# Two fillers fewer at the start, a k step of four more blocks ahead of a transpose, and token tiles 8-11 taken in pairs for three feature blocks

## The chip, the cores and the metric

The kernel runs on one NeuronCore of a Trainium2 chip. The metric is the device time of one execution in microseconds; the time given for a kernel is the median of its runs. The core's engines are TensorE (PE, matrix multiplication, with PEld for the loading of its stationary operand), VectorE (DVE), ScalarE (ACT), GpSimd (POOL) and SyncE (SP, which issues most DMAs).

## The reference

The layer adds three things: the input, a linear attention block and a dense GELU block, both fed by the same layernorm.

```python
def _A_ref(x, wqkv, wo):                      # x: 1 x 2048 x 640, 32 heads of 20
    qkv = (x @ wqkv) ...                      # q, k, v
    phi = lambda t: jnp.where(t > 0, t + 1, jnp.exp(t)) + 1e-6
    pq, pk = phi(q), phi(k)
    kv = einsum("bhsd,bhse->bhde", pk, v);  z = einsum("bhsd->bhd", pk)
    o = einsum("bhqd,bhde->bhqe", pq, kv) / (einsum("bhqd,bhd->bhq", pq, z) + 1e-6)
    return o.reshape(B, S, D) @ wo
def _B_ref(x, w1, b1, w2, b2):                # w1: 640 x 1536, w2: 1536 x 640
    return gelu(x @ w1 + b1) @ w2 + b2
xn = layernorm(x)
return x + _A_ref(xn, A_wqkv, A_wo) + _B_ref(xn, B_w1, B_b1, B_w2, B_b2)
```

All arrays are bfloat16. There are 2048 tokens, so 16 token tiles of 128; the model width of 640 makes 5 k steps of 128 (`DT`), and the hidden width of 1536 makes 12 feature blocks of 128 (`JT`).

## The kernel before

A planner (`Planner`) records, for every engine, its instructions in the order in which the Python code issues them, and puts semaphore waits where one depends on another. So each engine, and each DMA queue (most transfers go through SP's), works strictly in the order of the source[...]. PSUM is used as a ring of eight banks: `take(1)` hands out the next one, `at(b)` sets the ring, and a unit of matmuls has to wait until the bank's former content is read.

**Start (lines 442-459).** `filler(n, w)` issues n matmuls of constants, w columns wide, whose results nobody reads: four of 512 columns first, then six matmuls (L445) that open banks 0 to 5 with a matmul of constants summing to zero, then six fillers of 128 columns. Meanwhile DVE and POOL compute the layernorm of token tile 0: `ln_half` (L351, statistics), `ln_aggr` (L359 on DVE, the power on POOL at L361) and `ln_norm` (L373). `transp2(0)` (L336) transposes tile 0 on PE, `copy2(0)` brings it to `xnT`, one part on ACT (L344), the other on DVE (L345).

**First product, xn @ W1 (lines 461-512).** A list `plan` orders the work on PE. Its entries are:

- `hk(t, n, jb, ks)` (L431): for n tiles from tile t, feature block jb and only the k steps in `ks`; used for tiles 0 and 1, whose 12 feature blocks stay open in banks 0 to 5, so that work can begin when only some of the weights W1 and one tile are there. The last k step of an odd block is followed by two GELUs on ACT (L438).
- "B1": a small transpose of the bias. "T1": the transposes of tile 1 (L336) and their copies, and then on DVE the statistics of tiles 2 and 3. "T2": the transposes of tile 2 (`transp`, L381), its copy on DVE (L389), `ln_norm(3)`, the transposing DMA of tile 3, and then `ln_rest`, which holds all the remaining layernorms (tiles 4 to 15) and the loads of x for tiles 8 to 15.
- `pack(t, ...)`, that is `h_pack` (L415): one tile, four feature blocks in one bank. `h_list(t, n, lo, hi)`, that is one `h_unit` (L400) for each feature block from lo to hi: n tiles from t at once, so matmuls n x 128 columns wide, five k steps, and one GELU (L404).

Tiles 3 to 15 are transposed not on PE but by a DMA on SP's queue (`xnT_dma`, L263), issued as soon as the tile is normalised. An `h_unit` waits for the transposed form of all the n tiles that it takes.

**After that.** The k projection and its positive map phi (L548, L554), the sums over tokens (L581, L590), the q projection (L634), the small products for kv and the denominators (L644 to L698), and the output (`out_mm` L755, `rem_mm` L766), whose results DVE adds to x and DMAs write out.

Of the kernel before, what the change touches and what calls it, by code (L numbers as in the profile page):

```python
# [7 lines left out]
P = 128  # L8
# [104 lines left out]
def bass_parallel_sum__linear_attn_block__dense_activation_gelu__prompt_kernel(  # L113
# [9 lines left out]
    JT = F // P  # L123
# [17 lines left out]
    with contextlib.ExitStack() as es:  # L141
# [59 lines left out]
        def take(n):  # L201
            b = ring[0]
            if n == 2 and b % 2:
                b += 1
            b %= 8
            ring[0] = (b + n) % 8
            return b

        def bank(b, lo=0, hi=512):
            return ps[:, b * 512 + lo: b * 512 + hi]  # L210
# [106 lines left out]
        def filler(n, w=512):  # L317
            b = take(1)
            Pl.ins(pe, [lambda e: e.matmul(bank(b, 0, w), nc.const_aps.tensor(1.0, [P, P], BF16),
                                           nc.const_aps.tensor(1.0, [P, w], BF16), start=True, stop=True)  # L320
                        for _ in range(n)], writes=[B_[b]])
# [25 lines left out]
        def ln_half(t, h):  # L347
            s = t % 4
            cut = XA if t == 0 else HW
            lo, hi = ((0, cut), (cut, D))[h]  # L350
            Pl.ins(v, lambda e: e.bn_stats(stats[:, s, 6 * h:6 * h + 6], x_in[:, t, lo:hi]),  # L351
                   reads=[r_x[t][min(h, len(r_x[t]) - 1)]], writes=[r_stats[s][h]])
            if h == 0:
                Pl.ins(g, lambda e: e.tensor_single_scalar(stats[:, s, 2:3], stats[:, s, 2:3], D * EPS, ALU.add),
                       reads=[r_stats[s][0]], writes=[r_stats[s][0]])
# [68 lines left out]
        def at(b):  # L424
            ring[0] = b
# [14 lines left out]
                        reads=[B_[b], r_b1c], writes=[r_HG[u][jb - 1 + i] for u in range(t, t + n)])  # L440

        at(6)
        filler(4)
        for b in range(6):
            Pl.ins(pe, lambda e, b=b: e.matmul(  # L445
                bank(b), nc.const_aps.tensor(1.0, [P, P], BF16), pm[:].broadcast_to((P, 512)), start=True, stop=False),
                reads=[r_pm], writes=[B_[b]])
        at(7)
        filler(6, P)
        ln_half(0, 0)  # L450
        ln_half(0, 1)
        ln_aggr(0)
# [8 lines left out]
        h_list = lambda t, n, lo, hi: [(t, n, jb) for jb in range(lo, hi)]  # L461
        k_list = lambda t, n, ks, lo=0, hi=JT: [(t, n, jb, ks) for jb in range(lo, hi)]
        pack = lambda t, lo, hi: [(t, jb) for jb in range(lo, hi, 4)]
        plan = k_list(0, 1, [0]) + ["B1"] + k_list(0, 1, [1]) + ["T1"] + k_list(0, 1, [2])
        plan += k_list(1, 1, [0]) + k_list(1, 1, [1]) + k_list(1, 1, [2]) + k_list(0, 2, [3], 0, 4) + ["T2"]
        plan += k_list(0, 2, [4], 0, 4) + k_list(0, 2, [3, 4], 4)
        plan += pack(2, 0, 8) + h_list(2, 2, 8, JT) + pack(3, 0, 8) + h_list(4, 2, 0, 7) + h_list(6, 2, 0, 7)
        plan += h_list(4, 4, 7, JT) + h_list(8, 4, 0, JT) + h_list(12, 4, 0, JT)

        def ln_rest():  # L470
            def out(t):
# [406 lines left out]
```

## Time and profile before

| what | value |
|---|---|
| time, median of 6 runs | 208.75 us (208.37 to 211.3) |
| the profiled execution's own time | 207.83 us |
| its span, first to last instruction | 206.1 us |
| PE busy | 200.4 us, 97% of the span |
| DVE, ACT, POOL busy | 108.4, 70.3, 34.0 us |
| granted TensorE clock, mean | 1.000 |
| fillers of 512 columns (L319) | 4, from 0.84 us |
| first k steps of tile 0 (L431) | from 6.21 us |
| transposes of tile 2 (L381) | from 11.16 us |
| units of four tiles from tile 8 on (L400) | from 34.92 us |
| first matmul of the k projection (L548) | 60.98 us |

Times are given from the start of the span. A row of the timeline has the start, the length, the engine, the line, the operation and its operands, how often it was repeated, and in brackets how long the engine had been idle before and what released it. A matmul's length is a model of its latency, and matmuls overlap; the pace of a stream is read from the distance of their starts. The chain of waits follows the program back from its last instruction: at each step to whatever released it. In the rows of waits, the times are idle times of the engine.

### The profile page before, as it was taken

Reading aid. Unit: us, or ns where it says so; the run is one execution under the profiler, and the core shown is the slowest. Engines: PE = TensorE matmul, PEld = TensorE weight load, DVE = VectorE, ACT = ScalarE, POOL = GpSimd, SP = SyncE. Lnnn points to the kernel's source line nnn. Section 1 sums busy time; section 2 is a strip of 40 time slices with the busy share of each in tenths; the row PEclk is TensorE's granted clock in tenths of the full one; section 3 lists DMA queues with packets and bytes.
Section 4 is the critical chain, followed back from the end, with each engine's and each line's share of the span. In section 5 each row is a group of like instructions: output and inputs, shape, how many; then the busy total and the mean of one; then the engine's idle time right before and its main releaser. Section 6 shows DMA issues by size and latency. Waiting matters only on the chain.

```text
span 206.1 us, 3326 instructions
## 1 busy us (share of the span) xinstructions
PE 200.4 (97%) x1213; PEld 103.9 (50%) x1230; DVE 108.4 (53%) x238; ACT 70.3 (34%) x136; POOL 34.0 (16%) x85
## 2 busy tenths in 40 slices
PE   8999997999999999999999999999999999999995
PEld 3899863444444444444546444544444444444443
DVE  3586199100005889499848888543613923513132
ACT  2169974666667555212153554400000000000000
POOL 3234065800000000799000200000000000000000
PEclk9999999999999999999999999999999999999999
DMA  6938755899920111100010000328995522102301
GB/s 182 390 100 92 195 153 111 104 350 312 373 101 0 25 25 25 25 3 0 0 32 5 0 0 0 105 33 180 315 241 128 127 76 54 51 25 51 78 29 51
DMA packets 34457, 21.37 MB, mean 104 GB/s; under 512 B 21384, under 2 KB 33800, under 8 KB 34440
## 3 DMA queue, kind: packets, MB, share of 16 engines
q1 hardware_dynamic: 30384, 17.54, 32.0%
q10 hardware_dynamic: 4056, 3.61, 6.4%
q8 instruction: 10, 0.16, 0.3%
q14 instruction: 7, 0.06, 0.1%
HBM read 13.08 MB, written 2.62 MB: 76 GB/s over the span
## 4 chain that ended last, share of the span: by engine, by line
PE 84%; DVE 7%; DMA 3%; POOL 2%; issue 1%; SPq 1%; ACT 1%; DVEq 0%
PE ps L755 28%; PE ps L400 13%; PE ps L634 10%; PE ps L548 8%; PE ps L581 8%; PE ps L766 7%; DVE stats L351 4%; PE ps L554 2%; PE ps L590 2%; DMA xPK<-in_A_x_dram 2%; DVE xn_tm L373 2%; POOL rstd L361 1%; DMA xnT<-xn_tm 1%; PE ps L445 1%; DVE aggr L359 1%
## 5 line engine op out<-in xcount | busy, mean ns | idle before, releaser
L755 PE MATMUL ps<-W,HG 128*128 128x512 bf16 (+2 forms) x200 | 43.5, 366 | 0.3 <-ACT Msb L670 0.2
L400 PE MATMUL ps<-xnT,W 128*128 128x512 bf16 (+1 forms) x232 | 41.5, 338 | 1.5 <-DMA xnT<-xn_tm 1.3
L404 ACT ACTIVATE HG<-ps,b1c 128x512 bf16<-128x512 f32 (+1 forms) x47 | 28.1, 638 | 13.7 <-PE ps L400 13.1
L400 PEld LDWEIGHTS ps<-xnT,W 128*128 128x128 bf16 x235 | 22.8, 98 | 19.6 <-issue 1.8
L755 PEld LDWEIGHTS ps<-W,HG 128*128 128x128 bf16 x204 | 19.5, 98 | 22.2 <-ACT Msb L670 0.2
L536 ACT ACTIVATE ek<-ps 128x512 bf16<-128x512 f32 x40 | 23.8, 597 | 19.4 <-PE ps L634 10.5
L537 DVE TENSOR_SCALAR ek<-ek 128x512 bf16<-128x512 bf16 x40 | 11.5, 288 | 29.6 <-ACT ek L536 29.6
L779 DVE TENSOR_TENSOR W<-ps,xnT 128x512 bf16<-128x512 f32 x15 | 10.4, 691 | 25.3 <-PE ps L755 19.4
L634 PE MATMUL ps<-xnT,Wqkv 128*128 128x512 bf16 x98 | 21.6, 379 | 0.1
L755 PE MATMUL ps<-Msb,PQ 128*128 128x512 bf16 (+2 forms) x84 | 19.5, 366 | 0.1
L351 DVE BATCH_NORM_STATS2 stats<-xPK 128x6 f32<-128x320 bf16 (+2 forms) x32 | 14.0, 479 | 7.5 <-DMA xPK<-in_A_x_dram 7.5
L548 PE MATMUL ps<-Wqkv,xnT 128*128 128x512 bf16 x78 | 17.8, 379 | 0.1
L575 POOL COPY Wqkv<-Wqkv 128x128 bf16<-128x128 bf16 x25 | 13.9, 558 | 22.4 <-PE ps L554 20.9
L581 PE MATMUL ps<-xPK,xn_tm 128*128 128x512 bf16 x78 | 17.3, 379 | 0.1
L634 PEld LDWEIGHTS ps<-xnT,Wqkv 128*128 128x128 bf16 x100 | 9.7, 98 | 11.5
L539 DVE SCALAR_TENSOR_TENSOR PQ<-ps,ek 128x512 bf16<-128x512 f32 x20 | 13.8, 692 | 2.1
L755 PEld LDWEIGHTS ps<-Msb,PQ 128*128 128x128 bf16 x85 | 8.2, 98 | 9.2
L548 PEld LDWEIGHTS ps<-Wqkv,xnT 128*128 128x128 bf16 x80 | 7.8, 98 | 9.4
L581 PEld LDWEIGHTS ps<-xPK,xn_tm 128*128 128x128 bf16 x80 | 7.8, 98 | 9.4
L539 DVE SCALAR_TENSOR_TENSOR xPK<-ps,ek 128x512 bf16<-128x512 f32 x16 | 11.1, 692 | 1.7
L604 DVE TENSOR_TENSOR Msb<-Msb,xPK 128x640 f32<-128x640 f32 x14 | 11.6, 825 | 0.5
L361 POOL TENSOR_TENSOR rstd<-aggr,mhalf 128x1 f32<-128x1 f32 x16 | 9.9, 619 | 8.2 <-DVE aggr L359 8.2
(79 smaller groups left out, 150.2 us busy)
## 6 DMA issues: line engine op xcount, KB each, us to landing
Wqkv<-in_A_wqkv_dram SPq DMA_DIRECT2D x3, 800.0 KB, 6.9
xnT<-in_A_x_dram SPq DMA_DIRECT2D x4, 512.0 KB, 7.0
W<-in_B_w_dram SPq DMA_DIRECT2D x5, 384.0 KB, 4.7
W<-in_B_w_dram SPq DMA_DIRECT2D x1, 1920.0 KB, 13.3
out_dram<-W ACTq DMA_DIRECT2D x15, 128.0 KB, 1.7
xn_tm<-rden ACTq DMA_DIRECT2D x12, 128.0 KB, 3.6
xPK<-in_A_x_dram SPq DMA_DIRECT2D x4, 320.0 KB, 4.8
Wo<-in_A_wo_dram SPq DMA_DIRECT2D x8, 160.0 KB, 9.0
```

What stands on the lines that cost most here:

```text
L351: Pl.ins(v, lambda e: e.bn_stats(stats[:, s, 6 * h:6 * h + 6], x_in[:, t, lo:hi]), reads=[r_x[t][min(h, len(r_x[t]) - 1)]], writes=[r_stat ...
L361: Pl.ins(g, lambda e: e.tensor_tensor(out=rstd[:, t:t + 1], in0=aggr[:, s, 1:2], in1=mhalf[:], op=ALU.pow), reads=[r_aggr[s], r_small], wr ...
L400: Pl.ins(pe, [(lambda e, k=k: e.matmul(bank(b, 0, w), W1[:, k, jb * P:(jb + 1) * P], xnT[:, k, tok], start=(k == 0), stop=(k == DT - 1))) ...
L404: Pl.ins(s_, lambda e: e.activation(HG[:, jb, tok], bank(b, 0, w), ACT.Gelu_apprx_tanh, bias=b1c[:, jb:jb + 1]), reads=[B_[b], r_b1c], wri ...
L536: Pl.ins(s_, lambda e: e.activation(e2, src, ACT.Exp), reads=br, writes=[r_ek[s]])
L539: Pl.ins(v, lambda e: e.scalar_tensor_tensor(out=d2, in0=src, scalar=0.0, in1=e2, op0=ALU.max, op1=ALU.add), reads=br + [r_ek[s]], writes= ...
L548: Pl.ins(pe, [(lambda e, k=k, b=b, t=t: e.matmul(bank(b), xnT[:, k, t * P:(t + 1) * P], Wqkv[:, k, D:D + MW], start=(k == 0), stop=(k == D ...
L575: Pl.ins(g, lambda e, k=k, i=i: e.tensor_copy(plain(Wqkv[:, k, D:2 * D], i), parts(Wqkv[:, k, 0:D], i)), reads=[r_Wq], writes=[r_Wk, r_WqP])
L581: Pl.ins(pe, lambda e, t=t, b=b, f=f, i=i: e.matmul(bank(b), xn_tm[:, t, f * P:(f + 1) * P], PK[:, t, 0:MW], start=(i == 0), stop=(i == NT ...
L634: Pl.ins(pe, [(lambda e, k=k, j=j, b=b: e.matmul(bank(b), Wqkv[:, k, D + j * P:D + (j + 1) * P], xnT[:, k, cc], start=(k == 0), stop=(k == ...
L755: Pl.ins(pe, [(lambda e, i=i, x=x, bk=bk: e.matmul(bank(bk, 0, x[1] - x[0]), seq[i][0], seq[i][1][:, x[0]:x[1]], start=(i == 0), stop=(i = ...
L766: Pl.ins(pe, lambda e, i=i: e.matmul(bank(b), seq[i][0], seq[i][1], start=(i == 0), stop=(i == NS - 1)), reads=seq[i][2], writes=[B_[b]], ...
```

## The change

Three edits, all in the order in which PE is given its work.

1. The first filler group has three matmuls of 512 columns, not four; the second has five of 128 columns, not six.
2. For tiles 0 and 1, the fourth k step (`[3]`) of feature blocks 0 to 7, not 0 to 3, stands ahead of "T2"; their fifth k step follows it, and blocks 8 to 11 get their last two k steps together, as blocks 4 to 11 did before.
3. For feature blocks 0 to 2, tiles 8 to 11 are taken as two units of two tiles (first 8 and 9 for the three blocks, then 10 and 11) and not as one unit of four. Blocks 3 to 11 follow in units of four. This is three units more, so what comes behind sits three banks further in the ring.

```diff
         at(6)
-        filler(4)
+        filler(3)
...
         at(7)
-        filler(6, P)
+        filler(5, P)
...
-        plan += k_list(1, 1, [0]) + k_list(1, 1, [1]) + k_list(1, 1, [2]) + k_list(0, 2, [3], 0, 4) + ["T2"]
-        plan += k_list(0, 2, [4], 0, 4) + k_list(0, 2, [3, 4], 4)
+        plan += k_list(1, 1, [0]) + k_list(1, 1, [1]) + k_list(1, 1, [2]) + k_list(0, 2, [3], 0, 8) + ["T2"]
+        plan += k_list(0, 2, [4], 0, 8) + k_list(0, 2, [3, 4], 8)
         plan += pack(2, 0, 8) + h_list(2, 2, 8, JT) + pack(3, 0, 8) + h_list(4, 2, 0, 7) + h_list(6, 2, 0, 7)
-        plan += h_list(4, 4, 7, JT) + h_list(8, 4, 0, JT) + h_list(12, 4, 0, JT)
+        plan += h_list(4, 4, 7, JT) + h_list(8, 2, 0, 3) + h_list(10, 2, 0, 3) + h_list(8, 4, 3, JT) + h_list(12, 4, 0, JT)
```

## The prediction

> **What bounds the kernel now.** The head of the page first.
>
> ```profile
> PE 200.4 (97%) x1213; PEld 103.9 (50%) x1230; DVE 108.4 (53%) x238; ACT 70.3 (34%) x136; POOL 34.0 (16%) x85
> PE 84%; DVE 7%; DMA 3%; POOL 2%; issue 1%; SPq 1%; ACT 1%; DVEq 0%
> ```
>
> TensorE (PE) is busy 97% of the 206.1 us and carries 84% of the chain that ended last; the 7% of VectorE (DVE) is not after it but before it, so there must be a stretch in which the layernorms lead. The waits of PE alone, over the first 36 us (engine, line, who released it: total, times, longest):
>
> ```profile
> PE ps L400 <- DMA xnT<-xn_tm: 1.3, 1, 1.3
> PE ps L319 <- PEq L863: 0.8, 1, 0.8
> PE ps L431 <- ACT xnT L344: 0.3, 1, 0.3
> ```
>
> There is one wait of size inside the stream. The timeline of PE from 20 to 36 us places it, and the chain of waits shows what ends it:
>
> ```profile
> 20.39 13.20 PE L400 MATMUL ps<-xnT,W 128*128 128x256 bf16 x94
> 34.92 1.24 PE L400 MATMUL ps<-xnT,W 128*128 128x512 bf16 x5 [1.33 <-DMA xnT<-xn_tm]
> ```
>
> ```profile
> 31.71 0.31 DVE xn_tm L373
> 32.02 0.03 DVE stats L351
> 32.05 2.63 DMA xnT<-xn_tm
> 34.68 0.25 issue
> ```
>
> The unit that starts at 34.92 is the first of `h_list(8, 4, 0, JT)`: it needs tiles 8 to 11 at once, and tile 11's transposing DMA, issued at 32.05, lands at 34.68. Back from there the chain runs through the layernorms (DVE, with a step on GpSimd, POOL) to 8.24 us, DVE's copy of tile 1's transposes. Behind 34.92 it is PE without a gap until the last rows.
>
> **How long the stall really is.** The 1.33 us counts from the modelled end of a matmul, which runs past the next one's start. Counted by starts: a 256-column step is 0.109 us (the timeline's L431 group of 20 from 11.44 to the next group at 13.62), a 512-column one 0.216 (20 of L548 in 4.32 us of chain). From 20.39: 14 units of two tiles (70 x 0.109 = 7.64) and 5 of four (25 x 0.216 = 5.39) end at 33.43. So 34.92 - 33.43 = **1.49 us** is the most that any reordering of the units here can recover, as long as tile 11 lands when it does and PE comes when it comes.
>
> **Edit 3, tiles 8-11 by two.** At 33.43 the new plan asks only for tiles 8 and 9. Their DMAs are the first two in the queue:
>
> ```profile
> 27.79 2.66 SPq L263 DMA_TRANSPOSE xnT<-xn_tm  x2
> ```
>
> With tile 11's delay from issue to landing (2.63) the second, issued near 29.2, is there by 31.9: 1.5 us early. Three units of tiles 8-9 are 15 matmuls x 0.109 = 1.64 us, so PE asks for tiles 10-11 at 35.07. Before, it could go on at 34.92, so 0.15 us of margin is left and no stall. Added work: 30 matmuls of 256 columns (3.28) in place of 15 of 512 (3.24): +0.04 us. Nine units of four follow as before. The stream is then 1.49 - 0.04 = **1.45 us** ahead.
>
> Here the Trainium skill speaks against the change. "TensorE: Matmul & The Clock Gate", Back-to-back issue gap, says that in a real stream with a weight load per matmul a 128-column matmul takes about 81 ns and a 512-column one about 131: far from proportional, so halving the width is dear. An estimate on a straight line between them gives 98 ns at 256 columns: 30 x 98 - 15 x 131 = +0.97 us, leaving 0.5 of gain. The trace has the very case, 70 such matmuls from 20.39 at 0.109 each, and the 512-column step at 0.216: I take the row, +0.04.
>
> ScalarE (ACT) gets six GELUs of 256 columns for three of 512. In the L438 group 12 take 4.49 us, 0.37 each, against 0.55 us of PE per unit: hidden. Every later unit lies three banks on in the ring of eight, and a unit still waits for the one eight places before; the two-bank takes skip an odd bank at other places, but PE shows no wait for a bank that this could lengthen. The added unit waits fall where data are long there: nothing. Tiles 12-15 are wanted about 1.45 us sooner, at 36.7 + 45 x 0.216 = 46.4; with 13 transposing DMAs, the last issued at 38.1 us, tile 15 lands near 40.7. Hidden.
>
> **Edit 1, two fillers fewer.** One cold 512-column matmul (six of them start from 2.50 to 5.02: 2.52/6 = 0.42) and one of 128 columns (0.35/6 = 0.06): 0.48 us of work that feeds nothing. Is it on the path? PE around it, and DVE's row for what comes next:
>
> ```profile
> 2.50 2.68 PE L445 MATMUL ps<-pm,const-bfloat16-1.0 128*128 128x512 bf16 x6
> 5.02 0.51 PE L319 MATMUL ps<-const-bfloat16-1.0 128*128 128x128 bf16 x6
> 5.37 0.57 PE L336 MATMUL ps<-ident,xn_tm 128*128 128x128 bf16 x5
> ```
>
> ```profile
> 4.91 0.34 DVE L373 TENSOR_SCALAR xn_tm<-xPK,aggr,rstd 128x256 bf16<-128x256 bf16 x1 [0.40 <-POOL rstd L361]
> ```
>
> Tile 0's first part is normalised at 4.91 + 0.34 = 5.25, its transposes start at 5.37 with some 0.05 to 0.1 between engines. So the fillers end just as the data arrive; without them PE idles about 0.25 to 0.4 us before 5.3. Gain 0 to 0.05; I take **0**. DVE sets the start, then ACT's copy (5.68 to 6.06) and the first k steps at 6.21.
>
> The other bound is the clock. The step falls from 0.105 us per 128 columns (a fourth of 0.42) to 0.058 at about 5 us. The skill's same page, section Part 1, says the clock is released after about 3.4 us of sustained work, seen through a free-running window, so the moment differs from run to run[...]. The row: unbroken work from 0.84, release near 5.0. After: nine matmuls of 512 end near 4.62 (0.84 + 9 x 0.42), five of 128 near 5.1 (three or four cold), so the run profiled would be released as before; by the rule the same for every phase that ends before 5.1. For a later phase both kernels hold idle gaps (the 0.27 before 6.21), the new one 0.1 to 0.4 more. If the window still counts, the shorter prelude helps: cold, the old fillers end at 5.67 (0.84 + 10 x 0.42 + 6 x 0.105), the new at 5.15, so tile 0 starts some 0.35 earlier. If it doesn't count, see rival C.
>
> **Edit 2, eight blocks' fourth k step ahead of tile 2's transposes.** Four more 256-column matmuls stand before "T2": 4 x 0.109 = 0.44 us moved, none added. What waits for T2 is DVE:
>
> ```profile
> 11.16 0.44 PE L381 MATMUL ps<-ident,xn_tm 128*128 128x128 bf16 x5
> ```
>
> ```profile
> 11.81 0.21 DVE L359 BATCH_NORM_AGGREGATE aggr<-stats 128x2 f32<-128x12 f32 x1
> 11.94 0.44 DVE L389 COPY xnT<-ps 128x640 bf16<-128x640 bf16 x1
> 12.78 0.45 DVE L373 TENSOR_SCALAR xn_tm<-xPK,aggr,rstd 128x640 bf16<-128x640 bf16 x1 [0.40 <-POOL rstd L361]
> ```
>
> The transposes end at 11.60, the copy starts at 11.94 behind the aggregate; it sits in DVE's wait for POOL, which the layernorm of tile 3 would have anyway until 12.78. Moved, the transposes end at 12.04; the copy, 0.04 behind them as for tile 1 (8.20 and 8.24), runs from 12.08 to 12.52, some 0.2 before 12.78. Behind it in DVE's order stands the whole layernorm chain with its DMAs on SP's queue, so past that 0.2 each tenth would reach tile 11's landing; inside it, nothing. The transposed tile 2 is needed by the packed units at 13.62. GELUs start 0.44 later (11.86 before) and ACT, busy 8.54 of the 9.2 us to 20.4, catches up later; the first bank it holds up would be needed over 1.5 us after it is free. The fifth k step, with its weights, comes later, not sooner. Cost **0**, bounds 0 and +0.3 us.
>
> **The sum.** -1.49 + 0.04 + 0 + 0 = **-1.45 us**. The profiled execution took 207.83 us (span 206.1 and 1.7 around it): 206.4. Against the median of 208.75, whose runs spread from 208.37 to 211.3: **207.3 us**, 0.7% less. A measurement of this kernel tells about 1% from no change, so I call it within 1%. If the layernorm chain keeps its times, PE cannot pass 34.92 with tiles 10-11, which caps the gain at 1.49 + 0.15 - 0.04 = 1.60 us.
>
> **Rivals.** A, the sum holds: 207.3, own range 206.8 to 207.8; chance 0.58.
> B, the stall comes back in small: tile 11 lands later against PE than here (T2's copy passes its 0.2, or the DMAs vary). Margin 0.15 us; a slip of 0.6 us costs 0.45: gain 1.0, 207.75. For: the margin is thin. Against: the chain has no other new wait. 0.14.
> C, slower: the clock's release is missed. PE's idle before 5.3 spoils the window, and the cold time is carried by tile 1's transposes ("T1", L336 at 7.76), on which DVE's chain at 8.24 waits. One window (3.4 us, the skill's figure) later: 24 k steps at 0.105 instead of 0.056 put T1 some 1.1 us back and all with it: 208.4, net -0.35. Two windows: the release comes near 11.8, some 45 k steps are cold by then, and T2 is 2.3 us late: 209.6. It decides against the change once T1 or T2 is more than 1.45 us late in most runs. For: the spread up to 211.3 shows that something of that size happens already. Against: work is unbroken for 4.2 us even so. 0.10, mostly within 1%.
> D, the late-release runs gain more: 0.35 us from the shorter cold prelude, and fewer of the 211 kind in the median: 206.5. For: the same spread. Against: the profile shows no such run. 0.14.
> E, the fillers' 0.48 us is gained too: the cap stands, 207.15. DVE's 5.25 speaks against it. 0.04.
>
> Faster by over 1% (below 206.66) needs D in strength: 0.15. Slower by over 1% needs C over two windows or a stall not seen here: 0.09. The rest, 0.76. The range takes in B, D and C's first window: 206.2 to 208.9.
>
> **What would show it.** In the changed profile PE's wait for the xnT DMA is gone or under 0.2 us; units of 256 columns run on to about 36.7 at 0.109; the first Wqkv matmul (60.98 now) starts near 59.5; T1 stays at 7.76, tile 11 still lands at 34.68; 128-column fillers end near 5.1 with an idle of about 0.2 us before L336. Wrong if T1 or tile 11's landing moves by over 0.2 us, or if PE is late behind 36.7.

## The result, and the profile after

| kernel | median | range | runs |
|---|---|---|---|
| before | 208.62 us | 207.75 to 211.32 | 65 |
| after | 206.99 us | 206.56 to 209.42 | 30 |

The ratio is 0.9933, 95% interval [0.9919, 0.9946]: 0.7% faster, 1.40 us by the ratio and 1.63 by the medians. Forecast were 207.3 us and a gain of 1.45. In a few executions of some of these kernels the mean granted clock is 0.992 instead of 1.000, and those of the kernel before then take some 2 us longer; where this blurs a comparison, the median over the runs at full clock is given too, called so.

The heads of the page after, busy time by engine and the chain that ended last:

```profile
PE 200.5 (98%) x1226; PEld 105.5 (51%) x1243; DVE 108.6 (53%) x238; ACT 70.6 (34%) x139; POOL 32.9 (16%) x85
...
PE 94%; DMA 2%; ACT 1%; issue 1%; SPq 0%; DVE 0%
```

DVE's share of the chain fell from 7% to nothing and PE's rose from 84% to 94%: in this execution the layernorms no longer lead anywhere. The waits of PE over the first 40 us (who waited for whom: total, times, longest), and PE's timeline from the first units of tiles 4-5 to the k projection (start, length, instruction):

```profile
PE ps L319 <- PEq L863: 0.8, 1, 0.8
PE ps L431 <- DMA W<-in_B_w_dram: 0.3, 1, 0.3
```

```profile
20.84 39.14 PE L400 MATMUL ps<-xnT,W 128*128 128x256 bf16 x226
59.82 2.54 PE L548 MATMUL ps<-Wqkv,xnT 128*128 128x512 bf16 x11
```

The wait of 1.3 us for the xnT DMA is gone, and line 400 is one unbroken group where there were two. The k projection of the kernel before starts in PE's timeline at

```profile
60.82 4.48 PE L548 MATMUL ps<-Wqkv,xnT 128*128 128x512 bf16 x19
```

(the 60.98 of the table ahead is the time in the chain of waits). From its first start to the first L548, line 400 takes 59.82 - 20.84 = 38.98 us; before, 60.82 - 20.39 = 40.43. That is **1.45 us less**, the forecast's sum.

Yet this execution took 206.82 us, against 207.83 for the profiled one of before: only 1.01 us less. The rest is at the start. The group begins 0.45 us later, 0.37 of it because the k steps of tile 0 began at 6.58 and not at 6.21:

```profile
4.64 0.74 PE L319 MATMUL ps<-const-bfloat16-1.0 128*128 128x128 bf16 x5
5.44 0.79 PE L336 MATMUL ps<-ident,xn_tm 128*128 128x128 bf16 x5
6.58 0.84 PE L431 MATMUL ps<-xnT,W 128*128 128x128 bf16 x12 [0.34 <-DMA W<-in_B_w_dram]
```

In this execution PE waited for the first block of W1, in that of before for ACT's copy. No edit touches the first loads, and the start differs between executions with the old fillers too: with edit 3 alone the same k steps began at 6.69.

### The profile page after: what moved, and what is told of

The parts are those of the page before. It is cut to its first block, busy times and chain, and to the rows that moved or that the text cites. A ratio compares the mean times of both kernels' runs of the same rounds, so it can differ in the third digit from the quotient of the medians.

```text
span 205.1 us, 3356 instructions
## 1 busy us (share of the span) xinstructions
PE 200.5 (98%) x1226; PEld 105.5 (51%) x1243; DVE 108.6 (53%) x238; ACT 70.6 (34%) x139; POOL 32.9 (16%) x85
## 4 chain that ended last, share of the span: by engine, by line
PE 94%; DMA 2%; ACT 1%; issue 1%; SPq 0%; DVE 0%
PE ps L755 29%; PE ps L400 20%; PE ps L634 10%; PE ps L548 8%; PE ps L581 8%; PE ps L766 7%; PE ps L431 3%; DMA W<-in_B_w_dram 2%; PE ps L415 2%; PE ps L590 2%; PE ps L554 2%; PE ps L644 1%; ACT Msb L670 1%; PE ps L698 1%; SPq L260 0%
## 5 line engine op out<-in xcount | busy, mean ns | idle before, releaser
L400 PEld LDWEIGHTS ps<-xnT,W 128*128 128x128 bf16 x250 | 24.3, 98 | 16.5
L548 PE MATMUL ps<-Wqkv,xnT 128*128 128x512 bf16 x80 | 17.9, 379 | 0.0
L575 POOL COPY Wqkv<-Wqkv 128x128 bf16<-128x128 bf16 x25 | 12.8, 514 | 22.4 <-PE ps L554 20.9
L548 PEld LDWEIGHTS ps<-Wqkv,xnT 128*128 128x128 bf16 x80 | 7.8, 98 | 9.4
```

The lines of the kernel that those rows point to most:

```text
L400: Pl.ins(pe, [(lambda e, k=k: e.matmul(bank(b, 0, w), W1[:, k, jb * P:(jb + 1) * P], xnT[:, k, tok], start=(k == 0), stop=(k == DT - 1))) ...
L548: Pl.ins(pe, [(lambda e, k=k, b=b, t=t: e.matmul(bank(b), xnT[:, k, t * P:(t + 1) * P], Wqkv[:, k, D:D + MW], start=(k == 0), stop=(k == D ...
L575: Pl.ins(g, lambda e, k=k, i=i: e.tensor_copy(plain(Wqkv[:, k, D:2 * D], i), parts(Wqkv[:, k, 0:D], i)), reads=[r_Wq], writes=[r_Wk, r_WqP])
```

## The experiments

Theory S: the stall ahead of tiles 8-11 is the whole gain, and edits 1 and 2 are worth nothing. Its rivals: F, the shorter prelude brings part; B, T2's place or the DMAs give the stall back; C, the clock's release is missed; and the estimate from the Trainium skill's figures, by which narrower matmuls are dear.

### Edit 3 alone

```diff
-        plan += h_list(4, 4, 7, JT) + h_list(8, 4, 0, JT) + h_list(12, 4, 0, JT)
+        plan += h_list(4, 4, 7, JT) + h_list(8, 2, 0, 3) + h_list(10, 2, 0, 3) + h_list(8, 4, 3, JT) + h_list(12, 4, 0, JT)
```

> The kernel before with edit 3 alone (tiles 8-11 by two for blocks 0 to 2). Theory S (the stall before tiles 8-11 is the whole gain): -1.45 us against the kernel before, ratio 0.993, and PE waits no longer for the xnT DMA. Theory F (part of the gain is the shorter prelude): -0.9 to -1.1 us, ratio 0.995.

Measured 206.84 us against 208.66 of before, run beside it, ratio 0.9887 [0.984, 0.9935], which leaves out theory F's 0.995; over runs at full clock 206.84 against 208.60, so 1.76 us. Its PE timeline:

```profile
20.87 39.14 PE L400 MATMUL ps<-xnT,W 128*128 128x256 bf16 x226
59.84 2.32 PE L548 MATMUL ps<-Wqkv,xnT 128*128 128x512 bf16 x10
```

59.84 - 20.87 = 38.97 us: the same stream as in the kernel after, with the old fillers and the old k steps. Edit 3 is the change.

### Edit 1 alone

```diff
-        filler(4)
+        filler(3)
...
-        filler(6, P)
+        filler(5, P)
```

> The kernel before with edit 1 alone (three and five fillers). Theory S: 0, ratio 0.9995 to 1.0005; the first transposes stay near 5.35 us, PE idles about 0.25 us before them, and the wait of 1.3 us for the xnT DMA stays. Theory F: -0.35 to -0.48 us, ratio 0.998. Rival C (the clock's release is missed more often): +1 us or more, ratio 1.005.

Measured 208.83 us against 208.66, ratio 0.9999 [0.9962, 1.0035]; at full clock 208.67 against 208.60. Zero within the interval, which leaves out rival C's 1.005 but is wide enough to hold theory F's 0.998; edit 3 alone already has the whole gain of the stream, so no more than the noise is left for F. The stall stands in PE's timeline as before, and somewhat longer:

```profile
35.35 26.06 PE L400 MATMUL ps<-xnT,W 128*128 128x512 bf16 x118 [1.57 <-DMA xnT<-xn_tm]
```

The idle of 0.25 us that was expected before the first transposes (5.43) did not come: the five fillers ran slowly and filled it.

### Edit 2 alone, and the change without edit 2

```diff
-        plan += ... + k_list(0, 2, [3], 0, 4) + ["T2"]
-        plan += k_list(0, 2, [4], 0, 4) + k_list(0, 2, [3, 4], 4)
+        plan += ... + k_list(0, 2, [3], 0, 8) + ["T2"]
+        plan += k_list(0, 2, [4], 0, 8) + k_list(0, 2, [3, 4], 8)
```

> The kernel before with edit 2 alone (the fourth k step of eight blocks ahead of tile 2's transposes). Theory S: 0 (bounds 0 and +0.3 us); DVE's copy of tile 2 starts near 12.08 instead of 11.94, and the layernorm of tile 3 stays at 12.78. Rival B: the layernorm of tile 3 and all behind it come later by 0.1 to 0.4 us, and so does the end, ratio 1.001 to 1.002.

Measured 208.36 us against 208.66, ratio 0.9966 [0.9936, 0.9996]; at full clock 208.36 against 208.60. That leans to a gain of 0.2 us, which no theory had. DVE's timeline shows where tile 2's copy (L389) went:

```profile
12.05 0.21 DVE L359 BATCH_NORM_AGGREGATE aggr<-stats 128x2 f32<-128x12 f32 x1
12.33 0.49 DVE L389 COPY xnT<-ps 128x640 bf16<-128x640 bf16 x1
13.01 0.45 DVE L373 TENSOR_SCALAR xn_tm<-xPK,aggr,rstd 128x640 bf16<-128x640 bf16 x1 [0.19 <-POOL rstd L361]
```

The copy starts 0.28 us behind the aggregate (0.13 before), and the layernorm of tile 3 still 0.96 behind it (0.97 before): the copy moved inside DVE's wait for POOL, which shrank from 0.40 to 0.19 us. So the same edit was taken out of the change, with the change itself run beside it:

> The changed kernel itself, beside the next two on one chip: 206.8 to 207.2 us, 1.4 to 1.7 us under the kernel before.

> The changed kernel with edit 2 undone (edits 1 and 3 alone). Theory S: the time of the changed kernel within 0.1 us. If the k steps moved ahead of tile 2's transposes bring part of the gain, 0.2 us or more slower than the changed kernel.

The changed kernel took 207.17 us (ratio to before 0.9918 [0.9898, 0.9938]), without edit 2 207.18 us (0.9921 [0.9904, 0.9938]). Edit 2 is worth nothing within about 0.6 us, as these two intervals go together; the 0.2 us above is not shown to be real.

### T2 far too late

All 24 matmuls of the fourth and fifth k steps stand ahead of T2.

```diff
-        plan += ... + k_list(0, 2, [3], 0, 8) + ["T2"]
-        plan += k_list(0, 2, [4], 0, 8) + k_list(0, 2, [3, 4], 8)
+        plan += ... + k_list(0, 2, [3, 4]) + ["T2"]
```

> The changed kernel with all the fourth and fifth k steps of tiles 0 and 1 ahead of tile 2's transposes, which so come 16 matmuls (1.75 us) later still. If the cover found for T2 (DVE's wait for POOL before the layernorm of tile 3, some 0.2 us) is real and finite, DVE's copy of tile 2 comes about 1.75 us later, the layernorm of tile 3 and the whole chain to tile 11 some 1.4 us later, and the time is 208.4 us. If T2's place costs nothing, 207.0 us.

Measured 208.60 us, ratio to before 1.001 [0.9993, 1.0028]: the whole gain is gone, 1.4 to 1.6 us against the changed kernel's 207.17 and 206.99. DVE's timeline:

```profile
12.15 0.21 DVE L359 BATCH_NORM_AGGREGATE aggr<-stats 128x2 f32<-128x12 f32 x1
14.47 0.49 DVE L389 COPY xnT<-ps 128x640 bf16<-128x640 bf16 x1 [2.11 <-PE ps L381]
14.88 0.44 DVE L373 TENSOR_SCALAR xn_tm<-xPK,aggr,rstd 128x640 bf16<-128x640 bf16 x1
```

Now DVE waits 2.11 us for PE's transposes, and the layernorm of tile 3 starts 2.73 behind the aggregate instead of 0.97, so 1.76 us later. The cover that edit 2 uses is real and it ends: edit 2's 0.44 us were free, the next 16 matmuls cost 1.4 to 1.6. Most of the price is not paid where the expectation had it, at the end of the chain to tile 11, but at once, in PE's own next steps (in this execution, which took 208.89 us):

```profile
15.02 2.41 PE L415 MATMUL ps<-xnT,W 128*128 128x128 bf16 x40 [0.59 <-DVE xnT L389]
18.06 1.16 PE L400 MATMUL ps<-xnT,W 128*128 128x256 bf16 x9 [0.63 <-DMA xnT<-xn_tm]
```

PE waits for tile 2's copy, then for tile 3's transposing DMA. By starts these two waits are 0.75 and 0.71 us; ahead of tiles 10-11 there are 0.43 more.

### One block by two instead of three

```diff
-        ... h_list(8, 2, 0, 3) + h_list(10, 2, 0, 3) + h_list(8, 4, 3, JT) ...
+        ... h_list(8, 2, 0, 1) + h_list(10, 2, 0, 1) + h_list(8, 4, 1, JT) ...
```

> The changed kernel with only one block of tiles 8-11 taken by two (h_list(8,2,0,1), h_list(10,2,0,1), then units of four from block 1). Theory S: one unit of tiles 8-9 covers 0.55 us of the 1.49 us stall, PE waits about 0.95 us (0.7 to 0.8 in the profile's modelled ends) before tiles 10-11, and the gain against the kernel before is 0.53 us: 208.1 us. If the size of the cover doesn't matter and the gain comes from the rest of the change, it stays at 207.0.

Measured 208.51 us, ratio 1.0003 [0.9968, 1.0039]; at full clock 208.32 against 208.56. The gain is 0.24 us, less than the 0.53 expected, and the interval holds both 0 and 0.53, so the times decide nothing here. PE's timeline has the rest of the stall where it should be, before tiles 10-11:

```profile
20.67 13.75 PE L400 MATMUL ps<-xnT,W 128*128 128x256 bf16 x99
35.27 25.53 PE L400 MATMUL ps<-xnT,W 128*128 128x256 bf16 x118 [0.85 <-issue]
```

By starts: 20.67 + 7.64 + 5.39 + 5 x 0.109 = 34.25, so PE stood for 1.02 us (0.95 expected). The k projection's first record, at 60.85, is one step of 0.216 late, since 19 steps and not 20 follow to the next line at 64.95; counted to 60.63, the stream is 39.96 us, 0.47 less than before. Three blocks cover the stall, one covers a third of it: it is the length of the work on tiles 8-9 that counts.

### What a narrower matmul costs

Tiles 12 to 15 by two as well, all 12 blocks, where nothing waits for data.

```diff
-        ... + h_list(12, 4, 0, JT)
+        ... + h_list(12, 2, 0, JT) + h_list(14, 2, 0, JT)
```

> The changed kernel with tiles 12-15 by two as well, for all 12 blocks: 120 matmuls of 256 columns for 60 of 512, where nothing waits for data. By the row (0.109 and 0.216 us a step): +0.14 us, 207.1 us. By the skill's figures (98 ns estimated on a line between 81 and 131): +3.9 us, 210.9 us.

Measured 207.72 us (6 runs, 206.94 to 208.04), ratio to before 0.9944 [0.9924, 0.9964], against the changed kernel's 0.9933: 0.2 us by the ratios, 0.7 by the medians. Far from 3.9. The timeline:

```profile
46.61 13.48 PE L400 MATMUL ps<-xnT,W 128*128 128x512 bf16 x121
```

One matmul of 512 columns and 120 of 256 lie between 46.61 and the next line's first record at 60.14. At 0.216 and 0.109 they make 13.30 of these 13.53 us. The rest is one missing record of 512 columns, the first of the next line (19 steps and not 20 follow from 60.14 to 64.24). A 256-column step took 0.109 here too. Counted to 59.92, the stream from 20.55 is 39.37 us, 0.39 more than in the changed kernel: 0.26 is a wait ahead of tiles 10-11 (35.48, asked for at 35.22), and 0.13 is left for the split, where the row gave 0.14.

### No fillers at all

Both `filler` lines of the changed kernel are removed.

> The changed kernel with both filler groups taken out altogether. PE works from about 1.1 to 3.7 us on the six matmuls that open the banks and then idles to 5.3. If the early release of the clock hangs on the fillers, 128-column steps stay at 0.107 us past the first k steps, tile 1's transposes come 1.1 us or more late, and the time is 208.1 to 209.5 us (+1.1 to +2.5 against the changed kernel). If they feed nothing at all, it stays at 207.0.

Measured 208.36 us, 1.2 to 1.4 us above the changed kernel. PE's timeline:

```profile
1.11 2.74 PE L444 MATMUL ps<-pm,const-bfloat16-1.0 128*128 128x512 bf16 x6 [1.11 <-DVE pm L287]
5.39 0.79 PE L336 MATMUL ps<-ident,xn_tm 128*128 128x128 bf16 x5 [1.54 <-DVE xn_tm L373]
...
8.08 1.46 PE L431 MATMUL ps<-xnT,W 128*128 128x128 bf16 x12
9.34 0.57 PE L336 MATMUL ps<-ident,xn_tm 128*128 128x128 bf16 x5
```

Tile 0's transposes start at 5.39, as with fillers: no filler is on the path to them. But the 12 k steps from 8.08 take 1.26 us, 0.105 each, where the changed kernel needs 0.057 (7.54 to 8.22): the pace is still that of the first fillers, and tile 1's transposes come at 9.34 instead of 8.22, 1.12 us late. This is the price that the prediction's rival C gave for one window (1.1 us). That the pace is a clock not yet released is read from the steps alone: the granted clock in the rows is 1.00 in this stretch, as it is from 0 to 5 us in the kernel before, where the steps are slow too (0.42 us for 512 columns). The two fillers taken out leave enough; all of them don't.

### The load of tile 1 from another queue

```diff
-        dma_x(1, 1)
+        dma(s_, x_in[:, 1, :], xv[P:2 * P, :], r_x[1])
```

> The changed kernel with the load of tile 1 issued from ACT's queue in place of SP's, so that the first block of W1, for which PE waits in the changed profile, is issued 0.43 us sooner (1.73 there). If that landing is what now leads, the first k steps start at 6.3 to 6.4 in place of 6.58 and the time falls by 0.1 to 0.3 us, 206.8 us; past that, ACT's copy of tile 0 (ended 6.26) leads. If the bytes on the way set the landing and not the issue, 207.0 us.

A miss: 208.94 us, ratio 0.9992 [0.9962, 1.0022]. The 12 runs scatter: four took 207.16 to 207.38, as the changed kernel does, the others 208.78 to 210.26. The profile is of the slowest, so what it shows is not shown for the rest. Its DVE timeline:

```profile
4.05 0.21 DVE L359 BATCH_NORM_AGGREGATE aggr<-stats 128x2 f32<-128x12 f32 x1
5.64 0.49 DVE L351 BATCH_NORM_STATS2 stats<-xPK 128x6 f32<-128x320 bf16 x1 [1.39 <-DMA xPK<-in_A_x_dram]
6.05 0.62 DVE L373 TENSOR_SCALAR xn_tm<-xPK,aggr,rstd 128x256 bf16<-128x256 bf16 x2
```

With W1's blocks issued ahead, tile 1 lands 1.4 us too late for DVE, whose order has tile 1's first statistics (5.64) ahead of tile 0's normalisation (6.05, 5.04 in the changed kernel). PE then idles from the fillers to 6.44, and its k steps are slow:

```profile
6.44 0.79 PE L336 MATMUL ps<-ident,xn_tm 128*128 128x128 bf16 x5 [1.07 <-DVE xn_tm L373]
...
8.90 1.46 PE L431 MATMUL ps<-xnT,W 128*128 128x128 bf16 x12
10.15 0.74 PE L336 MATMUL ps<-ident,xn_tm 128*128 128x128 bf16 x5
```

12 steps in 1.25 us is 0.104: the slow pace again, behind an idle of 1.07 us after the fillers, and tile 1's transposes are 1.9 us later than in the changed kernel. An idle of 0.65 us at this place (the profile of T2 far too late) left the steps at 0.057.

### Five blocks by two

```diff
-        ... h_list(8, 2, 0, 3) + h_list(10, 2, 0, 3) + h_list(8, 4, 3, JT) ...
+        ... h_list(8, 2, 0, 5) + h_list(10, 2, 0, 5) + h_list(8, 4, 5, JT) ...
```

> The changed kernel with five blocks of tiles 8-11 by two in place of three: PE asks for tiles 10-11 some 1.1 us later, so that a remaining stall of 0.1 to 0.3 us (seen in the run with tiles 12-15 split) can't come up. Theory S: a gain of 0 to 0.2 us against the changed kernel less 0.03 for the split, never slower by more than 0.1 us.

Measured 207.52 us, ratio 0.994 [0.992, 0.996], beside 207.17 of the changed kernel. By the medians that is 0.35 us slower, where at most 0.1 was expected, but the intervals overlap: inconclusive, and no better version. Its profile has no wait for xnT, though a load came late in it (x of tile 8, see rival B below), and its stream, 59.96 - 20.84 = 39.12 us, is only 0.14 longer than the changed kernel's.

### The load itself moved ahead

In the kernel before, the chain to tile 11 does not run through the layernorms alone, as the prediction has it. For 5.6 us, from 19.56 to 25.16, it runs through SP's queue and the load of x for tiles 8-9, for which DVE waits:

```profile
19.84 1.79 SPq L263
21.68 3.45 DMA xPK<-in_A_x_dram
```

So here is the kernel before, without any of the edits, but with x of tiles 8-11 loaded ahead of tile 4's transposing DMA.

```diff
+            dma_x(8, 2)
+            dma_x(10, 2)
             ln_stats(5)
             out(4)
...
             out(7)
-            dma_x(8, 2)
-            dma_x(10, 2)
             dma_x(12, 4)
```

> The kernel before, with none of the three edits, but with the loads of x for tiles 8 to 11 issued in SP's idle time between the transposing DMAs of tiles 3 and 4 (near 14.6 us) and not behind that of tile 7 (21.7 us). Theory S, and the reading that tile 11 is late because its load stands behind tile 7's transpose: DVE no longer waits 5.6 us for x, tile 11's transposed form lands near 29 us, no stall is left before the first unit of four, and the gain is 1.49 us or a little more (no matmuls are split): 206.9 to 207.1 us, with less spread from the load. If tile 11's landing is not what ends the stall, or the loads hold up the transposing DMAs of tiles 3 to 5 by as much, 208.2 to 208.6 us.

Measured 208.30 us (206.59 to 208.88), ratio 0.996 [0.9932, 0.9988]. PE's timeline:

```profile
18.63 2.40 PE L415 MATMUL ps<-xnT,W 128*128 128x128 bf16 x40
22.70 17.51 PE L400 MATMUL ps<-xnT,W 128*128 128x256 bf16 x114 [1.68 <-issue]
```

The stall ahead of tiles 8-11 is gone, as theory S says: one group runs on from 22.70 past the place. But a new one of 1.68 us has come up ahead of tiles 4-5. Their transposing DMAs now stand behind 640 KB of loads in the same queue; over 10 to 24 us the transposing DMAs take 4.1 us to land in the median, against 2.7 in the kernel before. In this execution (208.74 us) the gain turned into another wait. By the medians 0.37 us of it is left, by the ratio 0.83, and the fastest run, of which there is no profile, took 206.59.

## Why the prediction was right, and where it was not

**The sum.** Each term of the stream held. The stall of 1.49 us by starts, less 0.04 for the narrower steps: the stream is 1.45 us shorter in the changed kernel and 1.46 in edit 3 alone. To count by starts and not by the row's 1.33 us was right; the modelled ends would have given 1.29. Edit 1 is 0 (0.07 us at full clock, within some 0.7), edit 2 is 0 (0.01 us out of the change, within some 0.6). That it came out to the hundredth, and that the medians agree with it, is in part luck: the profiled execution of before was 0.8 us faster than the median of its 65 runs, the two profiled executions differ by only 1.01, and in other executions of the new order PE does wait (below).

**The signs.** The prediction named as a sign of being wrong that tile 1's transposes or tile 11's landing move by over 0.2 us. In the changed kernel's profile tile 1's transposes stand at 8.22 and not 7.76, tile 11's transposing DMA is issued at 32.51 and not 32.05, and the k projection starts at 59.98 in the chain's time and not near 59.5. The whole start of that execution was later, for PE and DVE alike, so the sum didn't suffer. The signs should have been counted from PE's start.

**The chain.** The prediction let the chain to tile 11 run through the layernorms only. It left out the load of x (19.56 to 25.16), and that is the part that varies, as rival B shows. Behind 34.92, where it has PE without a gap, the chain also leaves PE for 1.6 us from 131.40 (ACT, L670); the changed kernel has the same 1.6 us from 130.40.

**The row against the rule.** The estimate from the Trainium skill's figures ("TensorE: Matmul & The Clock Gate", Back-to-back issue gap) would have made the split cost 0.97 us and left a gain of 0.5. The row was the right choice, and the test with 120 narrow matmuls bears it out.

**The prelude.** "As released before" was too precise: in the changed kernel's profile five fillers of 128 columns take 0.74 us, where six took 0.51 before, so their pace was still the slow one, though the k steps had the fast one. In that execution it cost nothing, since PE then waited for W1. With edit 1 alone ACT's copy led, and the k steps began at 6.39 and not 6.21. But the old fillers can be slow as well: with edit 3 alone six of them take 0.84 us, and tile 0's transposes begin at 5.71, as the prediction reckoned for a cold prelude. What a later release costs is shown by the two kernels with a longer idle.

**Rival B was priced from one side.** It said that a slip of 0.6 us in tile 11's landing would cost 0.45 of the gain. Such slips are there. PE's timelines of the changed kernel run again, and of the one without edit 2:

```profile
35.91 4.39 PE L400 MATMUL ps<-xnT,W 128*128 128x256 bf16 x27 [0.43 <-issue]
```

```profile
36.53 3.74 PE L400 MATMUL ps<-xnT,W 128*128 128x256 bf16 x24 [0.96 <-issue]
```

In both, 110 matmuls of the group stand ahead of the wait (70, 25, and the 15 of tiles 8-9), so it is the wait for tiles 10-11: 0.60 and 1.13 us by starts. Yet on that chip the gain was 1.53 us.

The traces show where the slip arises. The wait follows the load of x for tile 8. Counted from PE's first unit of tiles 4-5, DVE takes it up after 4.77 us in the kernel before (wait of 1.49 by starts) and 5.03 with edit 1 alone (1.74), both in the old order. In the new order it is 4.78 in the changed kernel (no wait), 5.32 with tiles 12-15 split (0.26), 5.68 in the changed kernel run again (0.60) and 6.20 without edit 2 (1.13). The load stands behind tile 7's transposing DMA, which held SP's queue for 1.79, 2.00, 1.77, 2.42, 2.55 and 2.63 us in these six. With five blocks by two it was 6.29 (2.60 us on the queue), and the longer cover left some 0.1 us of wait.

So the failed step is the comparison: the slip was held against a kernel before that had none. With a slip of 0.26 us the old order's wait grew by 0.25, while the new order first uses up a margin. A slip that strikes both moves the gain up, towards the cap of 1.60, not down. That it strikes both alike is argued, not shown. No profile has the old order with a slip over 0.26. Tile 7's transposing DMA held the queue for at most 1.80 us in the three kernels that have the old fillers and the loads where they were, and for 1.77 to 2.63 us with the new fillers. Whether this is chance or edit 1 has a hand in it, nothing here decides.

**Rival D** (fewer late releases of the clock) stays open. It read them from runs near 211 us. Runs some 2 us above their kernel's median are 18 of 181 with the old fillers and 6 of 90 with the new ones (the run without fillers and the one with tile 1's load moved left out). Such counts don't tell the two preludes apart, and as no profile of such a run is kept, it isn't shown that they are late releases.

## What to carry to other kernels

When an in-order engine waits for the last of several tiles, put first the work that needs only the early ones, and size it by the stall counted from starts: here three blocks of 0.55 us for 1.49 us. Moving a step later on one engine is free only as long as its consumer has another wait to sit in; find that wait, and its length is the allowance (DVE's wait of 0.40 us here, of which edit 2 left 0.19; past it nearly all was paid). Follow the chain to the end of the stall through every queue: here its varying part was a load behind a transposing DMA. A delay that strikes both kernels must be charged to both, or a rival gets the wrong sign.

## What the runs showed of the hardware

With a new weight load for each matmul, the starts of matmuls of 128, 256 and 512 columns were 0.056, 0.109 and 0.216 us apart. In two executions in which PE stood for 1.07 and 1.54 us behind its first matmuls (in the second it had also done less work), its steps were still at 0.105 us per 128 columns past 9 us, where the changed kernel's were at 0.057 from 7.54 on. Transposing DMAs took 2.7 us to land in the median, and 4.1 with 640 KB of plain loads ahead of them in the queue (one execution each). Tile 7's held SP's queue for 1.76 to 2.63 us, where those of tiles 5 and 6 held it for 1.20.
